# Batch 0's v by heads, its attention between the scores, and two PSUM banks in one tile

## The chip, the cores and the metric

The kernel runs on one core of a Trainium2 chip. The metric is device time in microseconds (us), the median of several runs. Engines: TensorE (PE in the profile, PEld for its weight loads), VectorE (DVE), ScalarE (ACT), GpSimd (POOL) and SyncE (SP), each with its own instruction queue; SP, ACT and POOL also issue DMAs.

## The reference

Attention over 8 batches of 8 heads, 576 tokens, head size 64, each token seeing itself and the 127 tokens before it, with a linear bias by distance and head; then a feed-forward layer over all 4608 tokens.

```python
scores = scale * np.matmul(q, k.transpose(0, 1, 3, 2))          # 8 x 8 x 576 x 576
mask = (rel >= 0) & (rel < 128)
scores = np.where(mask, scores + bias[None], -1e9)
attn = softmax(scores)
x = np.matmul(attn, v)            # to 4608 x 512: tokens by heads
h = x @ w_in                      # 512 -> 2048
g = h * np.clip(h + 3.0, 0.0, 6.0) / 6.0
out = g @ w_out                   # 2048 -> 512, float32
```

## The kernel before

Work is counted in pairs `g` of heads: four pairs a batch, 32 in all. Tokens of a batch lie in five blocks of 128 (`NQ`, the last of 64). For a pair, q and k are transposed on TensorE so that the head size lies on partitions (`qTb`, `kTb`); TensorE makes the scores of each block with itself (`scd`, L324) and with the block before (`sco`, L356); ScalarE takes exponentials into `pd` and `po`; TensorE multiplies them with v (`av_matmuls`, L411 and L419), whose extra column of ones gives the row sums; VectorE takes reciprocals and multiplies (`avs`, L429 and L430 in the steady part, L440 and L441 or L452 and L453 in batches 0 and 1). `back` transposes `avs` into `xT`, the input of the feed-forward layer, on TensorE in the first batches and by DMA later.

The feed-forward layer runs over nine groups `nt` of 512 tokens. An up piece (`moe_up`) is four matmuls of 512 columns into `hps` (L492), then ScalarE's `r` (L516) and VectorE's product into `gbuf` (L517). There are 16 up pieces `ms` in a group; pieces 0 to 3 need the first quarter of `w_in`, 4 to 7 the second, and so on. A down piece (`moe_down`) is four matmuls into `ops` (L547); after four of them VectorE copies the 128 rows out (`osb`, L556) and SP stores them. `units` is the list of all pieces in order (in group 1 and later up and down pieces are mixed, by the strings in `ORDER`), and `fill(n)` issues the next `n`. A piece whose tokens are not attended yet is not issued.

All queues are written out by hand (`manual_schedule`): an engine runs its instructions in the order of the code. Semaphores between engines are laid by the framework, from which tiles and parts of tiles the instructions read and write. `first_batch` and `second_batch` issue batches 0 and 1; `segment` issues the pairs from 8 on, one pair's scores and exponentials interleaved with the `values` of the pair before, with `fill` between.

PSUM has eight banks: `ps_sc` two tiles of two banks (scores), `ps_h` two banks, and `ps_av` and `ps_o` one bank each. "av" holds what `values` makes, some transposes and some up pieces of group 0 (`UP_BANKS`); "o" holds the down pieces' sums, the transposes of `back` in batches 0 and 1, and some up pieces.

The start: q and k of pairs 0 and 1 come as 128 runs of nine tokens (`load_run`), transposed in 64x64 pieces (`transposes`, L231); pairs 2 and 3 come as `load_double`. v of batch 0 comes in five blocks of tokens (`load_block`), cast on POOL and VectorE (L193). The first quarter of `w_in` is loaded as float32 by SP (`load_raw`) and cast (`cast_raw`, L180); the other quarters are asked for by POOL (`load_w_in`, `second_w_in`), which converts on the way. ScalarE's queue also carries the k loads and one v block.

## Time and profile before

| | |
|---|---|
| median of 3 runs | 323.67 us (323.39 to 324.22) |
| span of the profiled execution | 321.8 us; the median of the runs lies 1.9 us above it |
| busy: PE, PEld, DVE, ACT, POOL | 308.2, 164.6, 175.5, 196.0, 138.4 us |
| granted clock | 1.000 |
| DMA packets | 131426, 52.43 MB; 118977 of them under 512 B |

A row of the page's groups reads: line, engine, operation, out<-in, shapes, count, then busy us and mean ns of one, then the idle time of the engine just ahead of it and what ended it. A timeline row reads: start, length, engine, line, operation, shapes, count, and in brackets the engine's idle time before it with what ended it. Matmul rows last longer than the time in which the next one starts: a 512-column matmul has 379 ns, but four take 0.86 us in a row.

### The profile page before, as it was taken

What the parts mean: (1) busy time and instruction counts of PE and PEld (TensorE: products, weight loads), DVE (VectorE), ACT (ScalarE), POOL (GpSimd) and SP (SyncE); (2) the same over time, 40 slices, a digit from 0 to 9 for tenths busy, and PEclk for the clock granted to TensorE, in tenths of its full rate; (3) what the DMA queues carried; (4) which work ended last, traced back from release to release, by engine and by line L of the source; (5) the groups of instructions that cost most, each with busy time, mean ns of one, the idle gap of its engine ahead of it and who ended that gap; (6) DMA issues with size and microseconds to landing.
All of it is one profiled execution on the core that took longest, in us unless ns stands there. A gap on an engine that the chain in (4) does not pass through costs nothing.

```text
span 321.8 us, 6865 instructions
## 1 busy us (share of the span) xinstructions
PE 308.2 (96%) x2620; PEld 164.6 (51%) x2659; DVE 175.5 (55%) x346; ACT 196.0 (61%) x337; POOL 138.4 (43%) x247
## 2 busy tenths in 40 slices
PE   6888999999999999999999999999999999999996
PEld 3564465455555545455667655455454444444443
DVE  6686595564346655555555556554655455445510
ACT  3857977877777766766676667666764344244401
POOL 7364590665494767446654663663331000000000
PEclk9999999999999999999999999999999999999999
DMA  7999999899999999999799999922011200000112
GB/s 273 262 369 210 269 233 214 235 200 189 201 256 170 242 200 189 204 202 230 179 214 207 211 189 202 236 66 89 20 55 59 80 34 34 33 33 35 65 49 83
DMA packets 131426, 52.43 MB, mean 163 GB/s; under 512 B 118977, under 2 KB 122817, under 8 KB 131393
## 3 DMA queue, kind: packets, MB, share of 16 engines
q1 hardware_dynamic: 125648, 46.15, 67.0%
q0 software_dynamic: 3696, 3.67, 7.0%
q10 hardware_dynamic: 2048, 2.16, 2.2%
q8 instruction: 21, 0.34, 0.5%
q14 instruction: 13, 0.10, 0.1%
HBM read 36.70 MB, written 9.44 MB: 143 GB/s over the span
## 4 chain that ended last, share of the span: by engine, by line
PE 83%; DMA 7%; ACT 4%; issue 2%; DVE 2%; POOL 1%; SPq 0%; ACTq 0%; DVEq 0%
PE ops L547 37%; PE hps L492 35%; DMA gbuf<-in_moe_w_in_dram 3%; PE scd L324 2%; DMA w_in_sb<-in_moe_w_in_dram 2%; PE av L419 2%; DMA ldbuf<-in_k_dram 2%; PE av L411 2%; ACT r L516 2%; PE sco L356 1%; PE ops L528 1%; DVE gbuf L517 1%; PE tp L254 1%; ACT gbuf L379 1%; ACT xT L479 1%
## 5 line engine op out<-in xcount | busy, mean ns | idle before, releaser
L517 DVE SCALAR_TENSOR_TENSOR gbuf<-r,hps 128x512 bf16<-128x512 f32 x144 | 98.5, 687 | 102.3 <-ACT r L516 99.4
L516 ACT ACTIVATE r<-hps,bias 128x512 f32<-128x512 f32 x144 | 98.8, 690 | 90.4 <-PE hps L492 89.3
L492 PE MATMUL hps<-xT,w_in_sb 128*128 128x512 bf16 (+1 forms) x622 | 143.3, 357 | 2.3 <-DMA w_in_sb<-in_moe_w_in_dram 0.9
L547 PE MATMUL ops<-w_out_sb,gbuf 128*128 128x512 bf16 x539 | 134.0, 379 | 2.4 <-issue 1.7
L492 PEld LDWEIGHTS <-w_in_sb 128*128 128x128 bf16 x640 | 59.0, 98 | 55.3 <-issue 1.7
L547 PEld LDWEIGHTS <-gbuf 128*128 128x128 bf16 x560 | 52.2, 98 | 56.9
L382 POOL TENSOR_SCALAR_AFFINE_SELECT pd<-pd 128x512 bf16<-128x512 bf16 x48 | 29.5, 631 | 37.8 <-ACT pd L379 37.7
L392 POOL TENSOR_SCALAR_AFFINE_SELECT po<-po 128x512 bf16<-128x512 bf16 x48 | 30.1, 633 | 32.6 <-ACT po L389 32.4
L556 DVE COPY osb<-ops 128x512 f32<-128x512 f32 x33 | 22.7, 688 | 22.0 <-PE ops L547 21.9
L379 ACT ACTIVATE pd<-scd,bias_d 128x512 bf16<-128x512 f32 x48 | 31.5, 684 | 4.7 <-PE scd L324 4.7
L389 ACT ACTIVATE po<-sco,bias_o 128x512 bf16<-128x512 f32 x48 | 33.1, 690 | 0.0
L206 POOL CAST tbuf<-ldbuf 128x512 bf16<-128x512 f32 (+1 forms) x45 | 25.5, 611 | 17.1 <-issue 17.1
L430 DVE TENSOR_TENSOR avs<-av,rc 128x384 bf16<-128x384 f32 (+1 forms) x48 | 23.6, 491 | 1.6
L419 PEld LDWEIGHTS <-pd 128*128 128x128 bf16 x192 | 14.3, 97 | 7.9 <-issue 0.5
L411 PE MATMUL av<-vbuf,po 128*128 128x65 bf16 x192 | 18.0, 193 | 0.0
L419 PE MATMUL av<-vbuf,pd 128*128 128x65 bf16 x192 | 17.3, 194 | 0.0
L411 PEld LDWEIGHTS <-po 128*128 128x128 bf16 x192 | 14.3, 98 | 2.9 <-DVE avs L430 0.5
L395 ACT ACTIVATE p4buf<-sco,bias_d 128x64 bf16<-128x64 f32 x48 | 15.6, 325 | 0.0
L199 POOL CAST vbuf<-ldbuf 128x1024 bf16<-128x1024 f32 x14 | 14.2, 1041 | 2.4 <-DMA ldbuf<-in_v_dram 2.4
L324 PEld LDWEIGHTS <-kTb 64*128 64x128 bf16 x256 | 7.3, 94 | 14.3 <-issue 10.0
L324 PE MATMUL scd<-qTb,kTb 64*128 64x128 bf16 x256 | 12.7, 219 | 1.9 <-ACT kTb L232 1.2
L239 POOL CAST pr<-ldbuf 128x576 bf16<-128x576 f32 x18 | 11.5, 671 | 2.0 <-DMA ldbuf<-in_k_dram 1.9
(107 smaller groups left out, 216.7 us busy)
## 6 DMA issues: line engine op xcount, KB each, us to landing
out_dram<-osb SPq DMA_DIRECT2D x33, 256.0 KB, 2.5
ldbuf<-in_v_dram SPq DMA_DIRECT2D x31, 256.0 KB, 5.0
ldbuf<-in_q_dram SPq DMA_DIRECT2D x20, 256.0 KB, 4.8
ldbuf<-in_k_dram SPq DMA_DIRECT2D x16, 256.0 KB, 4.6
ldbuf<-in_q_dram SPq DMA_DIRECT2D x12, 288.0 KB, 6.4
ldbuf<-in_k_dram SPq DMA_DIRECT2D x12, 288.0 KB, 6.7
w_out_sb<-in_moe_w_out_dram POOLq DMA_DIRECT2D x4, 512.0 KB, 10.0
w_in_sb<-in_moe_w_in_dram POOLq DMA_DIRECT2D x3, 512.0 KB, 8.6
```

Source lines behind the costliest of these rows:

```text
L206: nc.gpsimd.tensor_copy(out=tbuf[:m, :, j, :], in_=s[:m, j, :, :].rearrange("p (i e) d -> p i (e d)", e=2))
L324: nc.tensor.matmul(scd[:, e, ts(j, 128)], lhsT=kT[r, j, :], rhs=qT[r, j, :], start=first, stop=first or j == 3)
L379: nc.scalar.activation(out=pd[:, e, :, :].rearrange("p j c -> p (j c)"), in_=sc[:, e, :], func=ACT.Exp, bias=bias_d[:, h:h + 1], scale=scale)
L382: nc.gpsimd.affine_select(out=pd[:, e, :, :], in_=pd[:, e, :, :], pattern=[[0, 4], [1, 128]], channel_multiplier=-1, base=0, compare_op=AL ...
L389: nc.scalar.activation(out=po[:, e, :, :].rearrange("p j c -> p (j c)"), in_=sc[:, e, :], func=ACT.Exp, bias=bias_o[:, h:h + 1], scale=scale)
L392: nc.gpsimd.affine_select(out=po[:, e, :, :], in_=po[:, e, :, :], pattern=[[0, 4], [-1, 128]], channel_multiplier=1, base=-1, compare_op=A ...
L411: nc.tensor.matmul(out_av, lhsT=po[:, e, qt % 4, :], rhs=vb[:, qt - 1, h, :], start=True, stop=False)
L419: nc.tensor.matmul(out_av, lhsT=d, rhs=vb[:, qt, h, :], start=(qt == 0), stop=True)
L492: nc.tensor.matmul(hps[:, lo:hi], lhsT=w_in_sb[:, ks, ts(ms, 128)], rhs=xT[:, ks, ds(src, hi - lo)], start=(ks == 0), stop=(ks == n_ks - 1))
L516: nc.scalar.activation(out=r6, in_=hps, func=ACT.Relu, bias=bias3[:, 0:1], scale=1.0 / 6.0)
L517: nc.vector.scalar_tensor_tensor(out=gts[nt][:, ms, :], in0=r6, scalar=1.0, in1=hps, op0=ALU.min, op1=ALU.mult)
L547: nc.tensor.matmul(ops[nt, sub], lhsT=gts[nt][:, ms, ts(sub, 128)], rhs=w_out_sb[:, ms, :], start=(ms == 0), stop=(ms == n_ms - 1))
```

## The change

1. q and k of pairs 0 and 1 are loaded as 96 runs of six tokens (`load_lone`), both heads side by side, cast by VectorE, ScalarE and POOL in another order, and transposed two heads at a time: 12 transposes of 96 columns for each instead of 18 of 64x64.
2. v of batch 0 is loaded by heads: the last 64 tokens as before, and then one DMA for each head's first 512 tokens, all on SP. POOL casts it pair by pair; VectorE and ScalarE take no part.
3. `attend(0)`, `attend_split(1)` and `attend(2)` stand between the scores of pairs 2 and 3 and what follows them, not behind the last exponentials.
4. `ps_av` and `ps_o` become one pool `ps_vo` with one tile `vo` of two banks, taken once; `bank("av", ...)` and `bank("o", ...)` return its halves, everywhere in the kernel. `attend(0, vo)` and `attend(2, vo)` use both halves. The transposes of `back(0)` and `back(1)` go into a `ps_sc` tile.
5. On POOL, six memsets (`memsets_later`) move from the start to behind the casts of v; `second_w_in` moves ahead of the casts of the raw quarter, all four of which are now POOL's; `load_w_in(2)` and `load_w_in(3)` move ahead of preparing batch 1.
6. `fill(6)` issues six up pieces of group 0 ahead of batch 1's first transposes, where `fill(2)` stood behind them; three later `fill(2)` become `fill(1)`.

The diff, without what only renames:

```diff
-    ps_av = ctx.enter_context(tc.tile_pool(name="ps_av", bufs=1, space=bass.MemoryType.PSUM))
+    ps_vo = ctx.enter_context(tc.tile_pool(name="ps_vo", bufs=1, space=bass.MemoryType.PSUM))
     ps_h = ctx.enter_context(tc.tile_pool(name="ps_h", bufs=2, space=bass.MemoryType.PSUM))
-    ps_o = ctx.enter_context(tc.tile_pool(name="ps_o", bufs=1, space=bass.MemoryType.PSUM))
+
+    vo = ps_vo.tile([128, 2, 512], FP32, name="vo")
+
+    def bank(tag, shape, dt=FP32, padded=None):
+        if tag == "h":
+            return ps_h.tile(shape, dt, tag="h", name="hb", padded_shape=padded or shape)
+        flat = vo[:, ("av", "o").index(tag), :]
...
-    def load_run(g, nm, eng):
...
+    LP, LT = 96, 6
+
+    def lone(g, nm):
+        room, at = (ldbuf["qk".index(nm)], 0) if g == 0 else (ldbuf[3], "qk".index(nm))
+        return room[0:LP, ds(at * 2 * LT * D, 2 * LT * D)].rearrange("p (e t d) -> p e t d", e=2, t=LT)
...
+    def load_heads(b, nm, hp, eng):
+        for e in range(2):
+            h = 2 * hp + e
+            eng.dma_start(out=tokens(b, nm)[:, 0:4, h, :],
+                          in_=src_of[nm][b, h, 0:512, :].rearrange("(j p) d -> p j d", p=128))
...
+    def cast_heads(b, hp, copy):
+        copy(out=vbuf[b % 2][:, 0:4, ds(2 * hp, 2), 0:D], in_=ld[b, "v"][:, 0:4, ds(2 * hp, 2), :])
...
-            for t in range(RT):
-                for e in range(2):
-                    r = slice(e * D, (e + 1) * D)
-                    nc.tensor.transpose(tp[r, t, :], src[r, ts(t, D)], ident[r, r])
+            for t in range(LT):
+                nc.tensor.transpose(tp[:, t, :], src[0:LP, t, :], ident[0:LP, 0:LP])
...
     def values(g, qts):
-        av = ps_av.tile([128, 3, 2, W], FP32, tag="av", name="av", padded_shape=[128, 3, 2, 85])
+        av = bank("av", [128, 3, 2, W], FP32, [128, 3, 2, 85])
...
-                ops[nt, sub] = ps_o.tile([128, d_model], FP32, tag="o", name="ops")
+                ops[nt, sub] = bank("o", [128, d_model])
...
     def first_batch():
         prepare(0, (V, A))
-        load_block(0, "v", 1, nc.scalar)
-        for j in (4, 0, 2, 3):
-            load_block(0, "v", j, nc.sync)
+        load_block(0, "v", 4, nc.sync)
+        for hp in range(NP):
+            load_heads(0, "v", hp, nc.sync)
...
+        cast_v(0, 4, P)
+        for hp in range(NP):
+            cast_heads(0, hp, P)
+        memsets_later()
+        attend(0, vo)
         scores_diag(3)
-        cast_v(0, 4, P)
-        cast_v(0, 0, P)
-        cast_v(0, 1, P)
-        cast_v(0, 2, V)
-        cast_v(0, 3, V)
+        attend_split(1, ("h", "h"))
         scores_off(3)
         exp_full(3)
-        attend(0)
...
-        attend_split(1, ("av", "h"))
-        attend(2)
-        back(0, "o")
-        cast_raw(0, P)
-        cast_raw(1, P)
+        attend(2, vo)
+        pair = ps_sc.tile([128, 2, 512], FP32, tag="sc", name="backs")
+        place = [pair[:, i, :].bitcast(BF16)[:, 0:SP] for i in range(2)]
+        back(0, place=place[0])
+        back(1, place=place[1])
+        second_w_in()
+        for ks in range(n_ks):
+            cast_raw(ks, P)
+        load_w_in(2)
         attend(3)
-        cast_raw(2, A)
-        back(1, "av")
-        cast_raw(3, P)
-        prepare_double(1, 0, (P,), "k")
-        second_w_in()
+        prepare_double(1, 0, (P, V), "kq")
+        back(2, "o")
         up_begin(0, 0, 1)
         up_begin(0, 1, 1)
-        back(2, "o")
-        prepare_double(1, 0, (V,), "q")
         up_more(0, 0, 2)
         up_more(0, 1, 2)
         back(3, "av")
-        wide_double(1, 0, "k", V)
-        wide_double(1, 0, "q", A)
         up_more(0, 0, 3)
         up_more(0, 1, 3)
         done[0] = NP
-        fill(2)
+        fill(6)
+        wide_double(1, 0, "k", V)
+        wide_double(1, 0, "q", A)
+        load_w_in(3)
         prepare_double(1, 1, (P,), "k")
-        load_w_in(2)
         prepare_double(1, 1, (P,), "q")
-        load_w_in(3)
```

In the changed kernel's line numbers, the `values` matmuls are L435 and L443, their multiply L454, the up matmuls L516, the product L541, the down matmuls L570 and the `osb` copy L579.

More of the change, by code (lines that the diff above doesn't have):

```diff
@@ L71 @@
     ps_sc = ctx.enter_context(tc.tile_pool(name="ps_sc", bufs=2, space=bass.MemoryType.PSUM))
-    ps_av = ctx.enter_context(tc.tile_pool(name="ps_av", bufs=1, space=bass.MemoryType.PSUM))
+    ps_vo = ctx.enter_context(tc.tile_pool(name="ps_vo", bufs=1, space=bass.MemoryType.PSUM))
     ps_h = ctx.enter_context(tc.tile_pool(name="ps_h", bufs=2, space=bass.MemoryType.PSUM))
-    ps_o = ctx.enter_context(tc.tile_pool(name="ps_o", bufs=1, space=bass.MemoryType.PSUM))
+    vo = ps_vo.tile([128, 2, 512], FP32, name="vo")
[3 more added lines that the diff above has]
+        flat = vo[:, ("av", "o").index(tag), :]
+        if dt == BF16:
+            flat = flat.bitcast(BF16)
+        dims = (padded or shape)[1:]
+        n = 1
+        for d in dims:
+            n *= d
+        flat = flat[:, 0:n]
+        if len(dims) == 1:
+            return flat[:, 0:shape[1]]
+        if len(dims) == 2:
+            return flat.rearrange("p (a b) -> p a b", a=dims[0])[:, 0:shape[1], 0:shape[2]]
+        return flat.rearrange("p (a b c) -> p a b c", a=dims[0], b=dims[1])[
+            :, 0:shape[1], 0:shape[2], 0:shape[3]]
     tbuf = held.tile([128, NP, NQ, 128], BF16, name="tbuf")
@@ L85, with load_lone @@
     src_of = {"q": q, "k": k, "v": v}
-    runs = {nm: ldbuf[i][:, 0:NP * RT * D].rearrange("p (g c) -> p g c", g=NP)
-            for i, nm in enumerate("qk")}
-    def load_run(g, nm, eng):
-        b, hp = divmod(g, NP)
-        eng.dma_start(out=runs[nm][:, hp, :],
-                      in_=src_of[nm][b, 2 * hp:2 * hp + 2, :, :].rearrange(
-                          "e (p t) d -> (e p) (t d)", t=RT))
+    LP, LT = 96, 6
+    def lone(g, nm):
+        room, at = (ldbuf["qk".index(nm)], 0) if g == 0 else (ldbuf[3], "qk".index(nm))
+        return room[0:LP, ds(at * 2 * LT * D, 2 * LT * D)].rearrange("p (e t d) -> p e t d", e=2, t=LT)
+    def load_lone(g, nm, eng):
+        eng.dma_start(out=lone(g, nm).rearrange("p e t d -> p e (t d)"),
+                      in_=src_of[nm][0, 2 * g:2 * g + 2, :, :].rearrange(
+                          "e (a t) d -> a e (t d)", t=LT))
     def load_double(b, dp, nm, eng):
@@ L152, in warm_up @@
     def warm_up(n):
-        w = ps_av.tile([128, 4, 128], FP32, tag="av", name="w")
+        w = bank("av", [128, 4, 128])
         rhs = ident.rearrange("p (j c) -> p j c", j=1).to_broadcast([128, 4, 128])
@@ L217, in prepare @@
         for nm, copy in zip("qk", copies):
-            pr = prs.tile([128, RT * D], BF16, tag=f"pr{nm}", name="pr",
-                          padded_shape=[128, 2 * RT * D])
-            copy(out=pr, in_=runs[nm][:, g % NP, :])
+            pr = prs.tile([128, LT, 2 * D], BF16, tag=f"pr{nm}", name="pr",
+                          padded_shape=[128, RT, 2 * D])
+            copy(out=pr[0:LP, :, :].rearrange("p t (e d) -> p e t d", e=2), in_=lone(g, nm))
             st[g, nm] = pr
@@ L226, in transposes @@
             src = st.pop((g, nm))
-            tp = ps_h.tile([128, RT, RP], BF16, tag="h", name="tp", padded_shape=[128, 16, 64])
-            for t in range(RT):
-                for e in range(2):
-                    r = slice(e * D, (e + 1) * D)
-                    nc.tensor.transpose(tp[r, t, :], src[r, ts(t, D)], ident[r, r])
+            tp = ps_h.tile([128, LT, LP], BF16, tag="h", name="tp", padded_shape=[128, 8, 128])
+            for t in range(LT):
+                nc.tensor.transpose(tp[:, t, :], src[0:LP, t, :], ident[0:LP, 0:LP])
             copy(out=dst[:, hp, :, :].rearrange("p j c -> p (j c)")[:, 0:S].rearrange(
-                "p (a t) -> p a t", t=RT), in_=tp.rearrange("p t a -> p a t"))
+                "p (a t) -> p a t", t=LT), in_=tp.rearrange("p t a -> p a t"))
     def prepare_double(b, dp, copies, nms="kq", early=None):
@@ L244, in prepare_double @@
             st[b, dp, nm] = pr
-    BANKS = {"h": ps_h, "av": ps_av, "o": ps_o}
     def double(b, dp, nm, part, tag, copy):
@@ L250, in double @@
         t0, t1 = ((0, 5), (5, RT))[part]
-        tp = BANKS[tag].tile([128, t1 - t0, 128], BF16, tag=tag, name="tp2",
-                             padded_shape=[128, 8, 128])
+        tp = bank(tag, [128, t1 - t0, 128], BF16, [128, 8, 128])
         for t in range(t0, t1):
@@ L262, in double_begin @@
         for part, (t0, t1) in enumerate(((0, 5), (5, RT))):
-            tp = BANKS[tags[part]].tile([128, t1 - t0, 128], BF16, tag=tags[part], name="tp2",
-                                        padded_shape=[128, 8, 128])
+            tp = bank(tags[part], [128, t1 - t0, 128], BF16, [128, 8, 128])
             for t in range(t0, t1):
@@ L432, in values, with attend @@
             in1=rc[:, 0:nq, :, :].to_broadcast([128, nq, 2, D]), op=ALU.mult)
-    def attend(g):
-        wide = ps_sc.tile([128, 2, 512], FP32, tag="sc", name="wide")
+    def attend(g, wide=None):
+        if wide is None:
+            wide = ps_sc.tile([128, 2, 512], FP32, tag="sc", name="wide")
         av = wide[:, :, 0:NQ * W].rearrange("p e (j c) -> p e j c", j=NQ)
@@ L447, in attend_split @@
             nq = len(qts)
-            av = BANKS[tag].tile([128, 3, 2, W], FP32, tag=tag, name="av",
-                                 padded_shape=[128, 3, 2, 85])
+            av = bank(tag, [128, 3, 2, W], FP32, [128, 3, 2, 85])
             av_matmuls(g, qts, lambda qt, e: av[:, qt - qts[0], e, :])
@@ L460, in by_xbar, with back @@
         return g >= XB and g not in (XB + 2, XB + 3)
-    def back(g, tag=None):
+    def back(g, tag=None, place=None):
         b, hp = divmod(g, NP)
@@ L469, in back @@
             return
-        tag = tag or ("o" if b < 2 else "h")
-        tp = BANKS[tag].tile([128, SP], BF16, tag=tag, name="tb", padded_shape=[128, 1024])
+        tp = place if place is not None else bank(
+            tag or ("o" if b < 2 else "h"), [128, SP], BF16, [128, 1024])
         for j in range(NQ):
@@ L512, in moe_up @@
             tag = UP_BANKS.get(ms, "h") if nt == 0 else "h"
-            hps = BANKS[tag].tile([128, NT], FP32, tag=tag, name="hps")
+            hps = bank(tag, [128, NT])
         up_mms(nt, ms, n, n_ks, hps)
@@ L524, in last_rows @@
                                        (cut, d_model, "h", nc.vector.tensor_copy, nc.sync)):
-            ps = BANKS[tag].tile([128, hi - lo], FP32, tag=tag, name="ops",
-                                 padded_shape=[128, d_model])
+            ps = bank(tag, [128, hi - lo], FP32, [128, d_model])
             for ms in range(n_ms):
@@ L614, in first_batch @@
         scores_diag(0)
-        prepare(1, (P, V))
+        prepare(1, (V, P))
         transposes(1, (V, V))
@@ L627, in first_batch @@
         double_copy(0, 1, "k", 0, (A, A))
+        tables_diag(2)
+        tables_off(2)
         scores_diag(2)
@@ L630, in first_batch @@
         double_copy(0, 1, "k", 1, (V, V))
-        tables_off(2)
         scores_off(2)
         exp_full(2)
-        scores_diag(3)
-        cast_v(0, 4, P)
-        cast_v(0, 0, P)
-        cast_v(0, 1, P)
-        cast_v(0, 2, V)
-        cast_v(0, 3, V)
+        cast_v(0, 4, P)
[3 more added lines that the diff above has]
+        attend(0, vo)
+        scores_diag(3)
+        attend_split(1, ("h", "h"))
         scores_off(3)
         exp_full(3)
-        attend(0)
         for dp in range(2):
@@ L682, in second_batch @@
         exp_diag(NP + 0, 1)
-        fill(2)
+        fill(1)
         scores_off(NP + 0)
@@ L692, in second_batch @@
         exp_diag(NP + 1, 1)
-        fill(2)
+        fill(1)
         scores_off(NP + 1)
@@ L703, in second_batch @@
         exp_off_full(NP + 2)
-        fill(2)
+        fill(1)
         for i in range(0, 4):
@@ L790 @@
     with tc.manual_schedule(engines=every):
-        load_run(0, "k", nc.scalar)
-        load_run(0, "q", nc.sync)
-        load_run(1, "k", nc.scalar)
-        load_run(1, "q", nc.sync)
+        load_lone(0, "k", nc.scalar)
+        load_lone(0, "q", nc.sync)
+        load_lone(1, "k", nc.scalar)
+        load_lone(1, "q", nc.sync)
         load_double(0, 1, "k", nc.scalar)
@@ L798 @@
         memsets()
-        memsets_later()
         first_batch()
```

## The prediction

> **What bounds the kernel now.** I read the page's busy shares first, then the costliest groups.

> ```profile
> PE 308.2 (96%) x2620; PEld 164.6 (51%) x2659; DVE 175.5 (55%) x346; ACT 196.0 (61%) x337; POOL 138.4 (43%) x247
> ...
> L547 PE MATMUL ops<-w_out_sb,gbuf 128*128 128x512 bf16 x539 | 134.0, 379 | 2.4 <-issue 1.7
> ...
> L556 DVE COPY osb<-ops 128x512 f32<-128x512 f32 x33 | 22.7, 688 | 22.0 <-PE ops L547 21.9
> ...
> L430 DVE TENSOR_TENSOR avs<-av,rc 128x384 bf16<-128x384 f32 (+1 forms) x48 | 23.6, 491 | 1.6
> ```

> TensorE is the bound, and its down matmuls (L547) almost never wait: 2.4 us of idle in front of 134.0. The next view is busy time in stretches (columns: PE, PEld, DVE, ACT, POOL, granted clock, DMA share, GB/s).

> ```profile
> 60.00:120.00 60.00, 58.85 (x535) 30.94 (x542) 32.14 (x65) 43.06 (x81) 39.75 (x68) 1.00 1.15 213
> 120.00:180.00 60.00, 59.10 (x550) 35.05 (x557) 34.01 (x68) 40.23 (x75) 34.99 (x62) 1.00 1.01 203
> 180.00:240.00 60.00, 59.05 (x505) 31.28 (x511) 32.96 (x66) 39.41 (x74) 29.06 (x52) 1.00 0.66 134
> ```

> Only 3.0 us of TensorE idle in 180 us: any wait put on TensorE here lengthens the run one for one. The chain of waits, in order of time, shows that the start is different. It hangs on DMA:

> ```profile
> 9.90 9.09 DMA gbuf<-in_moe_w_in_dram
> ...
> 21.98 7.49 DMA w_in_sb<-in_moe_w_in_dram
> ```

> The first quarter of `w_in` lands at 19.0, the second at 29.47. That start is what the change's title speaks of. But the diff also lays two PSUM banks, until now two pools (`ps_av`, `ps_o`), into one tile `vo`, and every `values` and nearly every `moe_down` of the whole kernel goes through it. So the last view is the timeline of one pair in the steady part (start, length, what).

> ```profile
> 131.47 1.03 PE L492 MATMUL hps<-xT,w_in_sb 128*128 128x512 bf16 x4
> ...
> 132.54 0.69 ACT L516 ACTIVATE r<-hps,bias 128x512 f32<-128x512 f32 x1 [1.12 <-PE hps L492]
> ...
> 132.61 0.19 PE L419 MATMUL av<-vbuf,pd 128*128 128x65 bf16 x1
> 132.64 1.02 PE L547 MATMUL ops<-w_out_sb,gbuf 128*128 128x512 bf16 x4
> ...
> 133.26 0.69 DVE L517 SCALAR_TENSOR_TENSOR gbuf<-r,hps 128x512 bf16<-128x512 f32 x1 [1.70 <-ACT r L516]
> ...
> 133.86 0.19 DVE L429 RECIPROCAL rc<-av 128x6 f32<-128x6 f32 x1
> 134.09 0.56 DVE L430 TENSOR_TENSOR avs<-av,rc 128x384 bf16<-128x384 f32 x1
> ...
> 134.56 0.68 DVE L556 COPY osb<-ops 128x512 f32<-128x512 f32 x1
> ...
> 135.23 0.19 PE L411 MATMUL av<-vbuf,po 128*128 128x65 bf16 x1
> ```

> The last `values` matmul starts at 132.61, the next down piece at 132.64, while VectorE reads `av` until 134.09 + 0.56 = 134.65. Two engines in two banks, side by side.

> **The shared tile.** In the changed kernel as built, the semaphores show what one tile does. 46 down pieces (first matmul, L570) wait for the multiply of the `values` before them (L454), though that reads the other half of `vo`; in the kernel before, none waits for it, and 29 wait for the copy of their own bank (L556). 20 starts of `values` wait for the `osb` copy of the other half (L579); before, none. What lays the semaphores takes the tile as one. Matmuls run in order, so behind a waiting one stand the rest of its down piece and the next up piece, for whose `hps` ScalarE and then VectorE wait.

> Term A, values then down. In the pair shown the down piece would wait 134.65 − 132.64 = 2.01 us. The delay has a fixed chain: the up piece just ahead of `values` ends, ScalarE's L516 (0.69), VectorE's L517 (0.69), reciprocal (0.19), multiply (0.56); a stall of TensorE earlier on doesn't shorten it. In the batch whose values start at 197.7 the timeline gives, for its eight, multiply's end less next down piece's start: 2.00, 1.92, 0.28, 1.06, 2.00, 1.06, 0, 0.69: 9.0 us. Where it is small, an up piece (0.86) stands between. Added up over all 48 multiplies of L430: 43 are late, 52.1 us.

> Term B, down then values. Same sum for the copies of L556 and the next `av` matmul (above: 134.56 + 0.68 = 135.24 against 135.23): 19 late, 8.2 us.

> Term C, transposes of batches 2 and 3 that go to the "av" half. ScalarE's copies of them end 1.25 us (55.40 against 54.15), 0.75 and 0.75 us behind the start of the next down piece, and two second parts stand 0.74 us ahead of the end of an `osb` copy: 4.2 us.

> Restart: after VectorE's multiply ended at 20.81 + 0.82 = 21.63, TensorE's transpose started at 21.69, 0.06 us. 62 waits make 3.7 us (nothing if they overlap, 9 us at 0.15).

> **The start.** Pairs 0 and 1 by six tokens: casts of 768 instead of 576 elements a partition (VectorE 0.64 us, by length 0.85), and 24 transposes of 96 columns for 36 of 64x64 (36 took 0.78; by the 18 of 128 columns in 1.18, estimated 1.0): exponentials 0 to 0.6 us later. ScalarE loses its v load (0.39). The `attend`s ahead of scores push the fourth pair's exponentials from 17.2 to about 18.5. All that is covered: the first quarter of `w_in` still lands at about 19.0, since on SP's queue nine v loads of the same bytes stand before it where four did (and one on ScalarE's), and DMA, not the issues, is full there; batch 1's loads follow as before. A landing 1 us later is inside the bounds below. What gates is POOL's queue. v's last block is cast at 16.31 now; POOL would cast the last heads at about 16.3 to 16.9, run the six memsets that stood at 3.74 to 6.44 (2.7) to 19.6, ask for the second quarter at 19.7 instead of 21.98, then cast the raw quarter alone: 0.88 of issue and four casts at 0.58, done at 22.9 instead of 20.6. The second quarter lands 7.5 us after its issue, at 27.2: a lead of 2.3 us at piece 4.

> The lead is lost at once. `fill(6)` now stands ahead of both `wide_double`s, so their copies come behind ScalarE's and VectorE's work for pieces 4 and 5 (0.69 + 0.69) and nothing covers them: pieces done at 28.9, VectorE's kTb copy (1.35) ends near 31.7, TensorE idle since 30.0. Until now that gap was 0.34 us at 24.90. By piece 8 I make it 1 us behind. Then the tile again: piece 12 ("av") right behind piece 11 ("o") waits about 1 us for L541, and of batch 1's backs ("o") and transposes ("av") three wait for a ScalarE copy of the other half (0.64 to 0.77 and latency, 0.8 each). 1 + 1 + 2.4 + a covering piece lost with the last `fill`: about 5 us, 0 to 8.

> **Sum.** 52.1 + 8.2 + 4.2 + 3.7 + 5 = 73, less the 3.2 us of idle that stretches 60 to 280 already hold, which the new waits swallow: 70 us. Span 321.8 + 70 = 392; the runs' median 323.67 lies 1.9 us over the span, so 393 to 394.

> [...]

> **Rivals.** (1) Not slower: the two halves never make each other wait, and the earlier second quarter stays a lead. Price: 2.3 us at piece 4, so 321.4. It needs the shortfall per down piece under 0.05 us; the rows give 1.1 on average. For it: DMA is on the chain until 29.47. 0.03. (2) The halves don't wait, but the order in the start costs its 1 us and the lost cover about 2: 326.7. Same evidence against the first half. 0.05. (3) The waits bite and TensorE's clock falls with the gaps. If a third of the 177 us busy in 60 to 240 ran at half pace, 59 more: 452. Against: in 5 to 10 us TensorE is busy 3.53 of 5.00 with the clock granted at 1.00, and after the change it would be about 80% busy with gaps of 2.3 us at most. 0.05. [...]

> **How the numbers follow.** My forecast has 0.87. Its own bounds: VectorE 0.2 us less late in 43 places, and nothing lost in the start, gives 380; restarts of 0.15, 8 us in the start and no idle swallowed gives 405. The rivals lie outside and hold 0.13, so the range stays 380 to 405. A measurement here tells 0.3% (1 us) from no change. Faster holds rival 1, 0.03; same 0.01 between rivals 1 and 2; slower 0.96.

> **What would show it.** Right: L570 has some 55 us of idle in front, released by avs L454; `av` matmuls some 8 released by osb L579; PE 78 to 80% of the span with clock 9; a batch takes about 42 us where it took 32.5; the second quarter is asked for near 19.7 and scores of pair 4 start near 31.7. Wrong: L570's idle still a few us, or PE clock under 9 in the middle slices.

## The result, and the profile after

The changed kernel takes 400.0 us (median of 4 runs, 398.25 to 400.25), against 323.68 us (323.39 to 324.22) for the kernel before in the same call: 1.2332 times as long, with a 95% interval of 1.2298 to 1.2367, or 76.3 us more. The profiled execution's span is 398.1 us. (One execution, of `e2_shared`, ran disturbed and is left out of that kernel's numbers below.)

First the page of the changed kernel: the busy shares, then the down matmuls (L570), the multiply of the values (L454) and the values matmuls (L443).

```profile
PE 323.8 (81%) x2572; PEld 168.4 (42%) x2611; DVE 176.2 (44%) x344; ACT 196.9 (49%) x336; POOL 140.3 (35%) x250
...
L570 PE MATMUL vo<-w_out_sb,gbuf 128*128 128x512 bf16 x492 | 127.5, 387 | 50.3 <-DVE avs L454 45.2
...
L454 DVE TENSOR_TENSOR avs<-vo,rc 128x384 bf16<-128x384 f32 (+1 forms) x48 | 23.6, 491 | 1.6
L443 PE MATMUL vo<-vbuf,pd 128*128 128x65 bf16 x192 | 17.3, 193 | 4.4 <-DVE osb L579 4.4
```

VectorE's multiply is as long as it was (23.6 us in 48) and waits for as little. What is new stands in L570's last column: 50.3 us of TensorE idle where L547 had 2.4, 45.2 of it ended by that multiply. L443 has 4.4 us ended by the copy of a down piece's sum. TensorE's share falls from 96% to 81% in a longer span.

The stretches of the steady part (columns: PE, PEld, DVE, ACT, POOL, granted clock, DMA share, GB/s) show that the loss is spread evenly, and that the clock dips in two of the three.

```profile
60.00:120.00 60.00, 45.41 (x364) 22.76 (x365) 22.26 (x43) 32.03 (x60) 26.70 (x46) 0.94 0.67 143
120.00:180.00 60.00, 48.04 (x379) 23.30 (x385) 25.28 (x50) 29.39 (x56) 27.10 (x48) 0.97 0.90 169
180.00:240.00 60.00, 47.81 (x438) 29.49 (x444) 26.21 (x51) 31.50 (x59) 26.09 (x44) 1.00 0.70 140
```

TensorE is busy 45 to 48 us in 60, where it was 59. Now one wait, in the timeline of the changed kernel:

```profile
85.63 1.03 PE L516 MATMUL hb<-xT,w_in_sb 128*128 128x512 bf16 x4
...
86.87 0.19 PE L443 MATMUL vo<-vbuf,pd 128*128 128x65 bf16 x1
...
86.98 0.69 ACT L540 ACTIVATE r<-hb,bias 128x512 f32<-128x512 f32 x1
...
87.78 0.69 DVE L541 SCALAR_TENSOR_TENSOR gbuf<-r,hb 128x512 bf16<-128x512 f32 x1 [2.42 <-ACT r L540]
...
88.38 0.19 DVE L453 RECIPROCAL rc<-vo 128x6 f32<-128x6 f32 x1
88.61 0.56 DVE L454 TENSOR_TENSOR avs<-vo,rc 128x384 bf16<-128x384 f32 x1
...
89.22 1.60 PE L570 MATMUL vo<-w_out_sb,gbuf 128*128 128x512 bf16 x4 [2.15 <-DVE avs L454]
```

This is the chain that the prediction wrote down, link for link: up piece, L540, L541, reciprocal, multiply (ends at 89.17), and 0.05 us later the down piece, which in the pair of before started 0.03 us behind the last `values` matmul.

### The profile page after: what moved, and what is told of

It reads as the page before. It is cut to its first block, busy times and chain, and to the rows that moved or that the text cites. A ratio compares the mean times of both kernels' runs of the same rounds, so it can differ in the third digit from the quotient of the medians.

```text
span 398.1 us, 6775 instructions
## 1 busy us (share of the span) xinstructions
PE 323.8 (81%) x2572; PEld 168.4 (42%) x2611; DVE 176.2 (44%) x344; ACT 196.9 (49%) x336; POOL 140.3 (35%) x250
## 4 chain that ended last, share of the span: by engine, by line
PE 60%; DVE 15%; ACT 12%; issue 6%; DMA 3%; POOL 2%; SPq 1%; ACTq 0%; DVEq 0%; POOLq 0%
PE vo L570 27%; PE hb L516 22%; ACT r L540 8%; DVE gbuf L541 6%; DVE avs L454 5%; PE ops L570 3%; DMA ldbuf<-in_k_dram 2%; PE scd L348 2%; DVE osb L579 2%; DVE rc L453 1%; DMA ldbuf<-in_v_dram 1%; PE sco L380 1%; ACT po L413 1%; ACT kTb L281 1%; PE vo L279 1%
## 5 line engine op out<-in xcount | busy, mean ns | idle before, releaser
L570 PE MATMUL vo<-w_out_sb,gbuf 128*128 128x512 bf16 x492 | 127.5, 387 | 50.3 <-DVE avs L454 45.2
L540 ACT ACTIVATE r<-hb,bias 128x512 f32<-128x512 f32 x135 | 92.9, 689 | 144.6 <-PE hb L516 142.7
L541 DVE SCALAR_TENSOR_TENSOR gbuf<-r,hb 128x512 bf16<-128x512 f32 x135 | 92.8, 687 | 136.7 <-ACT r L540 135.4
L516 PE MATMUL hb<-xT,w_in_sb 128*128 128x512 bf16 (+1 forms) x589 | 135.2, 359 | 3.9 <-DVE gbuf L541 2.1
L570 PEld LDWEIGHTS <-gbuf 128*128 128x128 bf16 x560 | 54.1, 99 | 113.5 <-issue 60.7
L516 PEld LDWEIGHTS <-w_in_sb 128*128 128x128 bf16 x640 | 59.6, 98 | 60.0 <-issue 6.5
L579 DVE COPY osb<-vo 128x512 f32<-128x512 f32 x31 | 21.3, 688 | 39.4 <-PE vo L570 39.4
L454 DVE TENSOR_TENSOR avs<-vo,rc 128x384 bf16<-128x384 f32 (+1 forms) x48 | 23.6, 491 | 1.6
L443 PE MATMUL vo<-vbuf,pd 128*128 128x65 bf16 x192 | 17.3, 193 | 4.4 <-DVE osb L579 4.4
L443 PEld LDWEIGHTS <-pd 128*128 128x128 bf16 x192 | 14.3, 97 | 14.8 <-POOL pd L406 5.8
L435 PE MATMUL vo<-vbuf,po 128*128 128x65 bf16 x192 | 17.9, 193 | 0.2
L419 ACT ACTIVATE p4buf<-sco,bias_d 128x64 bf16<-128x64 f32 x48 | 15.5, 323 | 0.0
L435 PEld LDWEIGHTS <-po 128*128 128x128 bf16 x192 | 14.3, 98 | 2.5
L453 DVE RECIPROCAL rc<-vo 128x6 f32<-128x6 f32 (+1 forms) x48 | 8.8, 183 | 10.7 <-PE vo L443 10.7
```

Source lines behind the costliest of these rows:

```text
L435: nc.tensor.matmul(out_av, lhsT=po[:, e, qt % 4, :], rhs=vb[:, qt - 1, h, :], start=True, stop=False)
L443: nc.tensor.matmul(out_av, lhsT=d, rhs=vb[:, qt, h, :], start=(qt == 0), stop=True)
L454: nc.vector.tensor_tensor(out=st[g, "avs"][:, qts[0]:qts[0] + nq, :, :], in0=av[:, 0:nq, :, 0:D], in1=rc[:, 0:nq, :, :].to_broadcast([128, ...
L516: nc.tensor.matmul(hps[:, lo:hi], lhsT=w_in_sb[:, ks, ts(ms, 128)], rhs=xT[:, ks, ds(src, hi - lo)], start=(ks == 0), stop=(ks == n_ks - 1))
L540: nc.scalar.activation(out=r6, in_=hps, func=ACT.Relu, bias=bias3[:, 0:1], scale=1.0 / 6.0)
L541: nc.vector.scalar_tensor_tensor(out=gts[nt][:, ms, :], in0=r6, scalar=1.0, in1=hps, op0=ALU.min, op1=ALU.mult)
```

## The experiments

Ten kernels were run. In each the gain or loss is against the kernel before in the same call (medians 323.99 to 324.43 us).

**1 and 2. The tile alone, and everything but the tile.** `e1_split` is the changed kernel with two tiles for one (its two attends that use both banks make their reciprocals and multiplies bank by bank, in `attend_halves`); `e2_shared` is the kernel before with one tile for its two pools.

```diff
 e1_split
-    vo = ps_vo.tile([128, 2, 512], FP32, name="vo")
+    halves = {"av": ps_vo.tile([128, 512], FP32, name="va"), "o": ps_vo.tile([128, 512], FP32, name="oo")}
...
-        flat = vo[:, ("av", "o").index(tag), :]
+        flat = halves[tag][:, :]
...
-        attend(0, vo)
+        attend_halves(0)
```

> The changed kernel with the one tile of two banks replaced by two tiles of one bank each; everything in the changed start stays, except that the two attends in these banks make their reciprocals and multiplies per half. Theory (the shared tile costs about 65 us, the new start 0 to 8): 324 to 332 us, and the idle in front of the down matmuls falls from 50 us to a few. Rival (the new start, through the late scores of pair 4 or through TensorE's clock, sets the rest of the run back): above 380 us, with the idle in front of the down matmuls hardly changed.

```diff
 e2_shared
-    ps_av = ctx.enter_context(tc.tile_pool(name="ps_av", bufs=1, space=bass.MemoryType.PSUM))
-    ps_o = ctx.enter_context(tc.tile_pool(name="ps_o", bufs=1, space=bass.MemoryType.PSUM))
+    ps_vo = ctx.enter_context(tc.tile_pool(name="ps_vo", bufs=1, space=bass.MemoryType.PSUM))
+    vo = ps_vo.tile([128, 2, 512], FP32, name="vo")
...
-        av = ps_av.tile([128, 3, 2, W], FP32, tag="av", name="av", padded_shape=[128, 3, 2, 85])
+        av = bank("av", [128, 3, 2, W], FP32, [128, 3, 2, 85])
```

> The kernel before with its two one-bank pools laid into one tile of two banks and nothing else changed: its own start, its own order. Theory: the waits between the halves come back without the new start: 62 to 76 us over the kernel before, so 386 to 400 us; about 50 us of idle in front of the down matmuls, ended by the multiplies of the values, and about 5 in front of the values matmuls. Rival (the start is what costs): within 5 us of the kernel before.

Measured: `e1_split` 330.08 us, 1.0175 (1.0145 to 1.0205), 5.7 us over the kernel before. `e2_shared` 392.19 us, 1.2077 (1.2029 to 1.2126), 67.8 us over. Both lie in the range of the first expectation. The page of `e1_split`, busy shares and the down matmuls, and then the stretch 120 to 180:

```profile
PE 314.3 (96%) x2611; PEld 165.8 (50%) x2611; DVE 175.6 (53%) x348; ACT 196.4 (60%) x336; POOL 139.9 (43%) x250
...
L580 PE MATMUL oo<-w_out_sb,gbuf 128*128 128x512 bf16 x512 | 127.3, 379 | 0.0
```

```profile
120.00:180.00 60.00, 60.00 (x553) 33.83 (x552) 32.72 (x65) 39.17 (x73) 34.76 (x61) 1.00 1.12 204
```

The waits are gone to the last tenth, with the changed start still in place. The groups of `e2_shared`, whose start is that of before, have them:

```profile
L560 PE MATMUL vo<-w_out_sb,gbuf 128*128 128x512 bf16 x512 | 129.6, 384 | 48.3 <-DVE avs L445 45.4 <-ACT kTb L272 2.8
...
L434 PE MATMUL vo<-vbuf,pd 128*128 128x65 bf16 x192 | 17.3, 193 | 4.4 <-DVE osb L569 4.4
```

What follows: the tile costs 67.8 us by itself and the rest of the change 5.7, together 73.4 of the 76.3 us. Two engines read and write the two banks side by side in `e1_split`, with 0.0 us of idle in front of the 512 matmuls of L580, and TensorE is busy for all 60.00 us of the stretch shown; it is the semaphores laid for one tile that ask for the waits.

**3 to 5. Where the 5.7 us of the start come from.** Each undoes one part of the change on top of `e1_split`.

```diff
 e3_order
         back(3, "av")
+        wide_double(1, 0, "k", V)
+        wide_double(1, 0, "q", A)
         up_more(0, 0, 3)
         up_more(0, 1, 3)
         done[0] = NP
-        fill(6)
-        wide_double(1, 0, "k", V)
-        wide_double(1, 0, "q", A)
+        fill(2)
...
 second_batch, three times
-        fill(1)
+        fill(2)
```

> The two-tile version of the changed kernel (measured 330.1 us against 324.4 for the kernel before), with one part of the change undone: both wide_doubles stand again ahead of the third up_more, two fills follow them instead of six, and the four fills go back to the second batch. Theory (the start costs through this order, since the kTb copy then has no pieces to hide behind): 324 to 326 us, and the scores of pair 4 start at 27 to 29 instead of 34.5. Rival (the earlier part of the start sets it, the six-token pairs, the attends ahead of scores, or the clock that opens later): 329 to 331 us.

```diff
 e4_mem
         memsets()
+        memsets_later()
         first_batch()
...
-        memsets_later()
         attend_halves(0)
```

> The two-tile version with one part undone: the six memsets stand at the start again, so POOL asks for the second quarter of w_in some 2 us sooner, near 18.3 instead of 20.4. Theory of the prediction (the landing follows the ask): it lands near 27.8 instead of 29.8 and the time falls by 1 to 2 us, to 328 to 329. Rival (the DMA engines are full from 15 to 29, so a sooner ask only lies longer in flight): it lands within 0.5 us of 29.8, and the time stays within 0.5 us of 330.

```diff
 e5_runs
-        load_lone(0, "k", nc.scalar)
-        load_lone(0, "q", nc.sync)
+        load_run(0, "k", nc.scalar)
+        load_run(0, "q", nc.sync)
...
 and prepare and transposes of the kernel before
```

> The two-tile version with one part undone: pairs 0 and 1 are again loaded as 128 half-runs of nine tokens and transposed by 36 small transposes a pair. Theory of the prediction (the six-token form costs at most 0.6 us and is covered): 329.5 to 330.5 us. Rival (the six-token form leaves TensorE less busy in the first 8 us, so that the full clock opens at 13.6 instead of 5.5): the full clock opens before 9 us and the time falls by 1 to 3 us.

Measured: `e3_order` 326.47 us, 1.0069 (1.0043 to 1.0094); `e4_mem` 328.97, 1.0141 (1.0121 to 1.0160); `e5_runs` 329.92, 1.0160 (1.0135 to 1.0185). The order is worth 3.5 us (5.7 less the 2.2 that `e3_order` still loses), the largest part: `e3_order` was expected at 324 to 326 us and is half a microsecond above that, with the scores of pair 4 at 27.76. They start at 24.90 in the kernel before, at 34.49 in `e1_split` and at 33.71 in the changed kernel, whose timeline shows what they wait for:

```profile
31.70 0.69 DVE L541 SCALAR_TENSOR_TENSOR gbuf<-r,vo 128x512 bf16<-128x512 f32 x1 [0.17 <-ACT r L540]
...
32.30 1.35 DVE L308 COPY kTb<-tp 128x1152 bf16<-128x1152 bf16 x1
...
33.71 0.40 PE L348 MATMUL scd<-qTb,kTb 64*128 64x128 bf16 x8 [1.76 <-DVE kTb L308]
```

The copy of kTb is queued behind the products of pieces 4 and 5, as the prediction said, and these now stand behind the second quarter's landing. The memsets are worth about 1 us by the medians, but the intervals of `e1_split` and `e4_mem` overlap; the ask went out 1.6 us sooner (18.80 against 20.39) and landed 1.1 sooner (28.68 against 29.77), between the two expectations, and the time is the first one's. The six-token form is worth nothing that can be told: `e5_runs` lies within 0.2 us of `e1_split`. The expectation's rival was half right: the full clock is granted from 6.98 us instead of 13.55, and the first `back` with a wait stands at 19.18 instead of 20.88; but then TensorE waits 2.12 us for a copy of `xT` and 1.85 for `w_in`, and the lead is gone.

**6. The sooner ask alone,** on the kernel before.

```diff
 e6_ask
         cast_v(0, 1, P)
+        load_w_in(1)
         cast_v(0, 2, V)
...
         prepare_double(1, 0, (P,), "k")
-        second_w_in()
```

> The kernel before with only the sooner ask: the second quarter of w_in is asked for right behind POOL's third cast of v, near 17, instead of at 21.98, with no wait for the probabilities of pair 1. Everything else is the kernel before. If the landing followed the ask (the prediction's sum): it lands near 24.5 and the time falls by 2 to 4 us, to 320 to 322. If the DMA engines are full: it lands at 28 to 29, at the cost of batch 1's loads, and the time stays within 1 us of the kernel before.

Measured: 324.67 us, 1.0015 (0.9998 to 1.0033). The ask went out at 15.18 and landed at 25.77, 3.7 us sooner than before, not the 28 to 29 of the second expectation; the time still is the second one's. But batch 1's loads fell behind: the first four of its k and q landed at 22.09, 23.61, 25.13 and 26.16, where the kernel before has 19.75, 20.50, 21.25 and 21.99. TensorE's timeline shows it in front of batch 1's transposes:

```profile
24.39 0.68 PE L282 MATMUL tp<-ident,pr 128*128 128x128 bf16 x9 [0.63 <-POOL pr L239]
27.00 1.14 PE L282 MATMUL tp<-ident,pr 128*128 128x128 bf16 x9 [1.93 <-DVE pr L239]
...
29.77 0.61 PE L324 MATMUL scd<-qTb,kTb 64*128 64x128 bf16 x8
```

So in this run what one load won, others lost; `e8_tail_ask` below shows the same, with these four loads at 19.86, 22.02, 23.31 and 24.88. Two cautions on this trace. It is of the slowest of the twelve executions (327.6 us against a median of 324.67), and from 27.02 to 30.43 it has the clock at half, and nine transposes take 1.14 us there, at 27.00, where nine at full clock, at 24.39, take 0.68. And the raw first quarter landed at 20.64 instead of 19.00, but it had been asked for at 10.96 instead of 9.90, ahead of the moved ask, so at least that 1.06 us is not the edit's doing.

The landing of the second quarter against its ask, read from the traces of all twelve kernels, one execution of each: asked at 15.18, 16.37, 18.76, 18.80, 20.16, 20.19, 20.39, 21.71, 21.98, 22.48, 23.27 and 24.12 us it landed at 25.77, 27.43, 29.05, 28.68, 28.99, 29.02, 29.77, 30.51, 29.47, 32.19, 30.50 and 32.00. The two earliest asks landed sooner than the rest; the seven between 18.76 and 21.98 all landed between 28.7 and 30.5, in no clear order. Two lines of the chain of waits, of `e4_mem` and of `e1_split`, show the ask and the flight:

```profile
18.80 9.89 DMA w_in_sb<-in_moe_w_in_dram
```

```profile
20.39 9.37 DMA w_in_sb<-in_moe_w_in_dram
```

The kernel before asked at 21.98 and waited 7.49.

**7 to 10. A version that might beat both.** All have two tiles, the early attends, 128 runs for pairs 0 and 1, the memsets at the start and the order of before. `e7_tail` asks for the second quarter behind the raw casts, `e8_tail_ask` ahead of them; `e9_blocks` loads v by blocks again; `e10_half` moves the raw quarter's ask up on SP's queue.

```diff
 e7_tail, on e5_runs, with e3_order's and e4_mem's edits
-        second_w_in()
-        for ks in range(n_ks):
-            cast_raw(ks, P)
-        load_w_in(2)
+        cast_raw(0, P)
+        cast_raw(1, P)
         attend(3)
-        prepare_double(1, 0, (P, V), "kq")
+        cast_raw(2, A)
+        cast_raw(3, P)
+        prepare_double(1, 0, (P,), "k")
+        second_w_in()
+        prepare_double(1, 0, (V,), "q")
...
-        load_w_in(3)
         prepare_double(1, 1, (P,), "k")
+        load_w_in(2)
         prepare_double(1, 1, (P,), "q")
+        load_w_in(3)
 e8_tail_ask: second_w_in() ahead of cast_raw(0, P)
 e9_blocks, on e7_tail: load_block and cast_v for load_heads and cast_heads
 e10_half, on e7_tail: load_raw() behind load_heads of pairs 0 and 1
```

> An attempt at a kernel that beats both: two tiles, v loaded by heads and the attends of pairs 0 to 2 early as in the changed kernel, the first two backs as there; but 128 half-runs for pairs 0 and 1, memsets at the start, the order of wide_doubles, fills, raw casts and w_in asks of the kernel before (second quarter asked behind the raw casts). If what is left of the start's cost (1.5 to 2 us after the order was undone) lies in POOL's order: 323.5 to 324.5 us, with the scores of pair 4 at 24 to 25. If it lies in the early attends or the loads by heads themselves: 326 us, as with the order alone undone.

> The same, but POOL asks for the second quarter ahead of the raw casts, near 19. If a sooner ask only lies longer in flight: it lands at 28.5 to 29.5 as all others asked between 18.8 and 22, and the time is within 0.7 us of the version that asks behind the casts. If the landing followed the ask: 1 to 2 us less than that version.

> The first attempt (325.5 us, 1.5 over the kernel before; its raw quarter is asked at 14.05 and lands at 21.14, against 9.90 and 19.00 in the kernel before) with v of batch 0 loaded and cast by blocks of tokens again, the attends still early. Theory (nine issues of v on SP, two a pair of heads, hold back the ask for the raw quarter): it is asked near 10, lands near 19, the scores of pair 4 start near 25, and the time is 323.5 to 324.5 us. Rival (the early attends cost): 325 to 326 us.

> The first attempt with the raw quarter of w_in asked for on SP behind the v of pairs 0 and 1, ahead of that of pairs 2 and 3. Theory (the place on SP's queue sets the landing): asked near 10 to 11, lands 19 to 20, v of pairs 2 and 3 1 to 2 us later, which nothing waits for yet: 323.5 to 324.5 us, perhaps under the kernel before. Rival (the DMA engines are full, so what one gains the other loses): 325 to 326 us.

Measured: 1.0047 (1.0031 to 1.0064), 1.0026 (1.0005 to 1.0048), 1.0038 (1.0020 to 1.0056) and 1.0066 (1.0039 to 1.0093), with medians 325.53, 325.54, 325.94 and 326.79 us. None beats the kernel before: by the medians they are 1.5, 1.5, 1.7 and 2.5 us over it. By `e9_blocks` it is not the loads by heads: there the raw quarter lands at 18.73, yet the time stays where `e7_tail` is, so the first expectation fell. `e10_half` brought the raw quarter in at 16.82, the soonest of all, and is no faster, above even its second expectation: its second quarter, asked at 22.48, landed at 32.19, and the later v of pairs 2 and 3, for which its expectation saw nothing waiting, held TensorE up for 1.43 us at 18.77. What keeps these versions over the kernel before is not settled. Among what they share are the early attends and the first two backs in one `ps_sc` tile, of which the second waits 0.73 us for a ScalarE copy in all four; neither was tried by itself.

## Why the prediction was right, point by point

The forecast was 393 to 394 us, and 400.0 was measured. Direction, mechanism and the largest term hold; the start was under-sized, the clock was put at nothing, and the sum for the steady part came near in part by luck.

**Terms A to C and the restarts: the mechanism right, the sum near in part by luck.** The prediction had 52.1 + 8.2 + 4.2 + 3.7, less 3.2 of idle swallowed: 65.0 us for the tile behind the start. The waits of the changed kernel from 60 to 340 us (total, times, longest):

```profile
PE vo L570 <- DVE avs L454: 45.2, 39, 2.2
PE vo L443 <- DVE osb L579: 4.4, 5, 1.2
PE vo L570 <- ACT kTb L281: 2.8, 3, 1.1
PE vo L279 <- DVE osb L579: 1.7, 2, 0.9
```

They are counted from the end of the matmul before; the prediction counted from the time at which the next one could have started, in Term A the start of the last `values` matmul plus the 0.03 us pitch, 0.16 us more for each. So Term A is 51.4 against 52.1. Term B was over-sized: 5.2 in 5 waits against 8.2 in 19, probably because the late down pieces themselves push the next copy and the next `values` apart. The last two rows are Term C, 5.3 against 4.2. Together that is 61.9 us, restarts included, against 68.2. Nor was the idle swallowed: from the first multiply of the steady part on, TensorE has 7 us of idle that these waits do not end, where the kernel before has 6.

By the profiled executions that part of the run, from the first multiply (66.11 us before, 75.32 in the changed kernel) to the end, became 67.2 us longer. That 65.0 lies so near is luck in part: the terms were some 6 us too large, less the 3.2 taken off, and the clock, at most 5.1, was left out. A batch takes 42.8 us (three in a row) where the prediction said 42. `e2_shared`, the tile alone, measured 67.8 (65.8 to 69.0 by its interval); in its profile 65.5 us of the loss come behind the first multiply.

**The start: under-sized, and one step of it failed.** The prediction's sum gave the start 5 us; in the profiles the first multiply of the steady part comes 9.2 us later (75.32 against 66.11). Of the 5 us, 3.4 are waits of the tile, which leaves 1.6 for the order and the lost cover; rival 2 prices the same two at 3. `e3_order` put them at 3.5, near the rival's price and twice the sum's, and `e1_split` measured 5.7 for all that is not the tile. The step that failed is the landings. The prediction took the 7.5 us of flight from the kernel before as fixed and so a lead of 2.3 us at piece 4, lost again later; the second quarter, asked at 20.16, landed at 28.99 and not at 27.2, so the lead was never more than 0.5, and the scores of pair 4 start at 33.71, not near 31.7. The raw quarter, asked at 12.89 instead of 9.90, landed at 20.11 instead of 19.00, the 1 us that the prediction left to its bounds. Whether the nine v loads ahead of it did that is open: `e2_shared` and `e6_ask`, with the v loads of the kernel before, have 20.29 and 20.64. That the six-token pairs are covered was right (`e5_runs`), though the count behind it was not: the traces have 24 transposes of 96 columns in the place of 72 of 64x64, 12 and 36 a pair.

**The clock: put at nothing.** The prediction held the clock at 1.00 and made its fall a rival of 452 us with 0.05. It fell, but little: three periods of 3.41 us between 60 and 180. At half pace that is 5.1 us of work lost, worked out from the rows and an upper bound, since no experiment took it away alone. The executions bear on it: the changed kernel took 399.85 to 400.25 us at a granted clock of 0.979 to 0.982 and 398.25 at 0.991. By clock and span (an estimate) the former lost 3.6 to 4.8 us more of work, and they took 1.6 to 2.0 us longer. So the clock is a part of the miss and not the largest: of the 6.4 us by which the sum was short, the profiles put 4.2 in the start and 2.2 behind it. `e1_split`, without the waits, has no such period from 14 to 300 us (a granted clock of 1.00 in every stretch), and `e2_shared` has two behind the start (0.94 from 60 to 120 us, 1.00 after it): of the 2.9 us that the two parts leave unexplained, the third accounts for at most 1.7. The other sign that the prediction gave for being wrong, L570's idle staying small, did not show; PE's share is 81% against 78 to 80.

**The rivals.** Not slower (321.4) and start alone (326.7) both needed the halves not to wait, and `e2_shared` shows that they do.

## What to carry to other kernels

In this case two PSUM banks in one tile were one thing to the semaphores: 45.2 us in 39 waits of the down pieces for the multiply that reads the other bank (60 to 340 us of the changed kernel), and 0.0 us of idle there with two tiles (`e1_split`). So before joining buffers, list which engine reads one part while another writes the other, and add up the start-to-end shortfalls from a trace in which they are apart; here that gave 65.0 us for the steady part, where 67.2 were added, with errors that partly cancelled. Where a load is asked for sooner while DMA is as busy as here (a DMA share of 1.15 from 15 to 29 us in the kernel before), don't take its flight time as fixed: asks at 18.80 (`e4_mem`) and 20.39 us (`e1_split`) had flights of 9.89 and 9.37, the one at 21.98 (the kernel before) had 7.49, and the ask moved to 15.18 (`e6_ask`) landed 3.7 us sooner with batch 1's first loads 2.3 to 4.2 us later. Where transposes or copies move behind work pieces on the same engines, look for the piece that covers them: the kTb copy of 1.35 us, queued behind two pieces' products, left TensorE waiting 1.76 us for it at 33.71 in the changed kernel; in the kernel before the wait ahead of the same scores was 0.34 us at 24.90.

## What the runs showed of the hardware

In the changed kernel's trace the granted clock changes at 7.61, 14.43, 89.53, 92.94, 103.18, 106.60, 120.25 and 123.66 us, between 1.00 and 0.50; the stretches between the changes are 6.83, 75.09, 3.41, 10.24, 3.41, 13.65 and 3.41 us, each close to a whole number of periods of 3.41. Stretches cut at borders of these periods (columns as above; the last but two is the granted clock):

```profile
99.77:103.18 3.41, 1.32 (x15) 0.71 (x14) 1.35 (x3) 3.37 (x7) 1.51 (x3) 1.00 1.28 226
103.18:106.60 3.42, 3.42 (x9) 1.23 (x9) 0.00 (x0) 0.62 (x2) 1.22 (x3) 0.50 0.05 19
147.55:150.96 3.41, 1.52 (x17) 0.86 (x15) 1.35 (x3) 2.05 (x4) 1.53 (x3) 1.00 0.00 0
150.96:154.38 3.42, 3.41 (x23) 1.51 (x21) 1.13 (x2) 1.16 (x3) 0.00 (x0) 1.00 0.13 49
```
